# Query weights loaded by eight DMAs of 16 rows each, every eighth partition, in place of one DMA of 128 rows

## The chip, the cores and the metric

The kernel runs on one core of a Trainium2 chip. The metric is the time of one execution on the device, in microseconds (us). A core has TensorE (PE), which multiplies matrices, VectorE (DVE), ScalarE (ACT), GpSimd (POOL) and SyncE (SP); SyncE does nothing here but issue transfers. Transfers run on 16 DMA engines beside the five. The on-chip memory has 128 partitions; a tile's row lies in one partition.

## The reference: one decode step of attention, then a gated feed-forward block

There are four sequences with one new token each, 512 features, 32 heads of 128, and a cache of 8192 keys and values for each head. All tensors are bf16.

```python
h  = x + attention(layernorm(x), k_cache, v_cache, wq, wo)
h2 = h + w_down @ (sigmoid(w_gate @ n) * (w_up @ n))     # n = layernorm(h)
# attention: q = layernorm(x) @ wq; softmax(q k^T / sqrt(128)) v; @ wo
```

The caches are 256 MB each, every byte is read once, and each is used for one query alone. The query weights wq are 512 x 4096, which is 4 MB.

## The kernel before, in words

The kernel is written engine by engine, with a list of operations for each engine and semaphores between them; nothing is reordered by a scheduler. A small helper class collects the lists: `emit` (line 41) adds an instruction with its waits, and `dma` (line 74) adds a transfer, which raises its semaphore by 16 when it has landed.

**Memory.** The largest tile, KV (line 126), has three slots of 64 KB in each partition. Slot 1 first holds x, slot 2 first holds wq, and slot 0 receives the first keys. Row p of wq's part of slot 2 is four consecutive rows of the matrix wq, 32 KB in one piece (line 179): partition p holds features 4p to 4p+3.

**Start.** ACT's queue loads x (line 178), and SyncE's queue loads wq (line 179). TensorE transposes x (line 227), VectorE, TensorE and ScalarE form the layer norm (lines 201 to 222), and TensorE projects the query with 128 small matmuls (line 239), once wq has landed. Line 249 spreads the query over partitions, line 255 copies it out, and GpSimd writes it, masked, into the left operand Lq (line 266).

**The main loop.** A group g is one sequence and four heads; there are 32. A key load (line 276) and a value load (line 290) bring 8 MB each, as 128 rows of 64 KB. VectorE transposes the keys in place in eight pieces (line 321), TensorE forms the scores (line 331), VectorE and ScalarE the softmax (lines 341 to 360), and TensorE multiplies with the values of the group before (line 370). Turns three to 31 of TensorE and VectorE run as a loop in hardware.

**Order of the transfers.** All but x go through SyncE's one queue, in this order: wq, keys 0, keys 1 (waits for the transposes of x, whose slot they take), values 0 (wait for the projection, as they take the slot of wq), keys 2, and then values and keys in turns, each waiting for the slot that it takes to become free (`load_k`, line 272, and `load_v`, line 278). The weights of the output projection and of the feed-forward block follow at the end (lines 298 to 315), and the result is stored last (line 512).

**End.** Output projection (line 409), second layer norm, gate and up projections (line 489), down projection (line 505), and a last transpose by matmul (line 510).

Of the kernel before, what the change touches and what calls it, by code (L numbers as in the profile page):

```python
# [88 lines left out]
def bass_sequential_preLN__mha_block_cached__glu_gated_glu__decode_kernel(  # L89
# [13 lines left out]
    _, H, S, DH = A_k_cache.shape  # L103
    F = B_w_gate.shape[1]
    assert DH == 128 and H == 32 and D == 512 and F == 14 * 128 and B == 4 and S == 8192
    NDC = D // 128
# [3 lines left out]
    SLOT = 4 * S * DH // 128  # L110
# [5 lines left out]
    prog = _Prog()  # L116
    emit = prog.emit

    with ExitStack() as es:
        def SB(name, shape, dt, **kw):  # L120
            return es.enter_context(nc.sbuf_tensor(name, shape, dt, **kw))

        def raw(t):
            return t.tensor if hasattr(t, "tensor") else t

        KV = SB("KV", [128, 3, SLOT], BF16, align_bytes=256)
# [29 lines left out]
        KVROW = 3 * SLOT  # L156

        def kv(slot, off, inner, p0=0, np_=128):
            return bass.AP(raw(KV), p0 * KVROW + slot * SLOT + off, [[KVROW, np_], *inner])
# [10 lines left out]
        for k in keys:  # L170
# [5 lines left out]
            "h (p r) d -> (h p) (r d)", p=32)  # L176

        t_x = prog.dma("act", "x", lambda e: e.dma_start(x_bf, A_x.rearrange("b s d -> (b s) d")))
        t_wq = prog.dma("sp", "wq", lambda e: e.dma_start(
            kv(2, 0, [[1, NDC * H * DH]]), A_wq.rearrange("(p c) f -> p (c f)", p=128)))  # L180

        t_id0 = emit("pool", lambda e: e.memset(ident[:, :], 0.0))
        t_ident = emit("pool", lambda e: e.affine_select(
# [386 lines left out]
```

## Time and profile before

| | |
|---|---|
| median of three runs | 1278.9 us (1278.86 to 1279.51) |
| profiled execution, first to last instruction | 1277.6 us |
| the profile's mean transfer rate | 431 GB/s over the span |
| read from the chip's main memory | 550.77 MB |
| mean granted TensorE clock | 0.912 of full speed |
| VectorE transposing keys (L321) | 568.6 us in 256 instructions |
| TensorE matmuls of scores (L331) | 543.2 us in 2048 |
| TensorE matmuls with values (L370) | 433.2 us in 1984 |

The runs' time includes what lies around the span; of the profiled execution itself the span is what is recorded, 1.3 us under the median of the runs.

How to read the profile. It is taken from one execution by the hardware. Its slices cut the span into 40 equal parts and give each engine's busy share in tenths; the row "DMA" gives the mean busy share of the 16 DMA engines. The queue table names the queues: q1 is SyncE's, q10 is ACT's, q8 and q14 fetch instructions and tables. A packet is one contiguous row that one DMA engine moves, or the small write that reports the end of a DMA on one engine. The stretches table takes parts of the span that the reader chooses and gives for each its bounds, its length, each engine's busy time and number of instructions, the granted clock, the DMA share (1.00 is all 16 engines) and the rate in GB/s; a packet counts whole in the stretch in which it starts. Timeline rows begin with start and length in us, and end with what ended the engine's idle time. "SPq" is SyncE's queue of instructions.

### The profile page before, as it was taken

The numbers are of one execution on the slowest core, as the hardware profiler recorded it, in microseconds if no ns is written. First come the engines' busy times: TensorE is split into PE (matmuls) and PEld (weight loads), VectorE is DVE, ScalarE is ACT, GpSimd is POOL, SyncE is SP. The second block draws the span as 40 slices with busy tenths as digits, with TensorE's granted clock in tenths as the row PEclk, the third lists the DMA queues.
The fourth block names the chain that finished last, engine by engine and source line by source line (L and its number), as shares of the span: only waits on it lengthen the run. The fifth ranks groups of instructions, "written<-read, shape, count | busy, mean of one in ns | idle before, by whom it ended". The sixth has DMA issues, their size and how long they took to land. (4 is left out here: it accounts for less than half of the span.)

```text
span 1277.6 us, 11138 instructions
## 1 busy us (share of the span) xinstructions
PE 1002.2 (78%) x4553; PEld 416.0 (33%) x4553; DVE 698.6 (55%) x729; ACT 84.8 (7%) x204; POOL 20.6 (2%) x84
## 2 busy tenths in 40 slices
PE   1598777779777788777788777797777797777898
PEld 1233323333223333223333333333233333333335
DVE  0855665446655446654456654456654466554461
ACT  0000000000000000000000000000000000000010
POOL 1000000000000000000000000000000000000000
PEclk9899888899888898888998888998888998889987
DMA  9999999999999999999999999999999999999998
GB/s 423 429 424 433 427 446 429 431 435 433 439 429 437 429 443 431 435 431 437 437 429 435 433 439 431 435 431 441 433 431 435 433 437 431 437 429 441 431 427 352
DMA packets 11605, 550.95 MB, mean 431 GB/s; under 512 B 1220, under 2 KB 1480, under 8 KB 2888
## 3 DMA queue, kind: packets, MB, share of 16 engines
q1 hardware_dynamic: 11584, 550.77, 99.6%
q8 instruction: 8, 0.13, 0.0%
q14 instruction: 5, 0.04, 0.0%
q10 hardware_dynamic: 8, 0.00, 0.0%
HBM read 550.77 MB, written 0.00 MB: 431 GB/s over the span
## 5 line engine op out<-in xcount | busy, mean ns | idle before, releaser
L321 DVE STREAM_TRANSPOSE KV<-KV 128x2048 uint32<-128x2048 uint32 x256 | 568.6, 2279 | 381.6 <-DVEq L52 381.6
L331 PE MATMUL PS<-KV,Lq 128*128 128x512 bf16 x2048 | 543.2, 416 | 259.1 <-PEq L52 258.4
L370 PE MATMUL PS<-KV,PT 128*128 128x512 bf16 x1984 | 433.2, 379 | 0.0
L331 PEld LDWEIGHTS PS<-KV,Lq 128*128 128x128 bf16 x2048 | 199.5, 104 | 602.2 <-issue 443.2
L370 PEld LDWEIGHTS PS<-KV,PT 128*128 128x128 bf16 x1984 | 193.9, 98 | 234.4
L347 ACT ACTIVATE E_sb<-PS,TS 128x512 bf16<-128x512 f32 x32 | 22.0, 688 | 1124.9 <-DVE TS L346 1124.9
L341 DVE TENSOR_REDUCE TS<-PS 128x1 f32<-128x512 f32 x32 | 22.1, 692 | 70.4 <-DVEq L52 70.4
L354 ACT ACTIVATE PT<-ET 32x256 bf16<-32x256 bf16 x128 | 53.0, 414 | 30.9 <-DVE ET L350 28.5
L350 DVE STREAM_TRANSPOSE ET<-E_sb 128x512 bf16<-128x512 bf16 x32 | 22.8, 711 | 30.7 <-DVEq L52 30.7
L396 DVE STREAM_TRANSPOSE OX<-PS 128x512 f32<-128x512 f32 x32 | 21.7, 677 | 21.0 <-PE PS L384 12.3
L266 POOL TENSOR_TENSOR Lq<-q_all,mask 128x16 bf16<-128x16 bf16 x32 | 8.4, 264 | 574.9 <-DVE TS L346 563.3
L270 POOL COPY OT<-OTs 128x4 bf16<-128x4 bf16 x30 | 5.8, 194 | 623.6 <-DVE OTs L399 623.6
L384 PE MATMUL PS<-KV,PT 128*128 128x512 bf16 x64 | 14.0, 379 | 0.0
L239 PE MATMUL PS<-xnT,KV 128*128 128x4 bf16 x128 | 3.6, 166 | 9.3 <-DMA KV<-in_A_wq_dram 9.3
L342 DVE STREAM_TRANSPOSE TS<-TS 128x32 f32<-128x32 f32 x32 | 6.8, 212 | 4.7
L359 DVE STREAM_TRANSPOSE TS<-TS 128x32 f32<-128x32 f32 x32 | 6.8, 211 | 4.7
L346 DVE STREAM_TRANSPOSE TS<-TS 128x32 f32<-128x32 f32 x32 | 6.8, 211 | 4.7
L399 DVE TENSOR_SCALAR OTs<-Or,small 128x4 bf16<-128x4 f32 x30 | 6.9, 229 | 4.5 <-DVEq L52 0.6
L384 PEld LDWEIGHTS PS<-KV,PT 128*128 128x128 bf16 x64 | 6.3, 98 | 7.5
L344 DVE TENSOR_SCALAR TS<-small 128x32 f32<-128x32 f32 x32 | 5.8, 181 | 5.0 <-DVEq L52 0.6
L358 DVE COPY TS<-small 128x32 f32<-128x32 f32 x32 | 5.8, 181 | 4.7
L398 DVE TENSOR_REDUCE Or<-OX 128x4 f32<-128x16 f32 x32 | 5.7, 179 | 4.7
(68 smaller groups left out, 77.0 us busy)
## 6 DMA issues: line engine op xcount, KB each, us to landing
KV<-in_A_v_cache_dram SPq DMA_DIRECT2D x2, 4096.0 KB, 27.4
KV<-in_A_wq_dram SPq DMA_DIRECT2D x1, 4096.0 KB, 12.3
KV<-in_A_wo_dram SPq DMA_DIRECT2D x1, 3072.0 KB, 22.5
KV<-in_B_w_gate_dram SPq DMA_DIRECT2D x1, 1792.0 KB, 28.2
KV<-in_B_w_up_dram SPq DMA_DIRECT2D x1, 1792.0 KB, 23.7
KV<-in_A_wo_dram SPq DMA_DIRECT2D x1, 1024.0 KB, 24.6
KV<-in_B_w_down_dram SPq DMA_DIRECT2D x1, 1024.0 KB, 23.1
KV<-in_A_k_cache_dram SPq DMA_DIRECT2D x32, 32.5
```

The costliest lines, as they stand in the source:

```text
L266: emit("pool", lambda e: e.tensor_tensor(dst, src, msk, ALU.mult), [t_q, t_mk, t_lq0, t_a5.get(g - 1), t_oc.get(g - 3)], key="lq")
L321: emit("dve", lambda e: e.transpose(v, v), key="tp", take=take, keep=keep)
L331: ins = e.matmul(S_b[0], Lq[:, hp, 15 - s:15 - s + 128], rhs, start=(s == 0 and hp == 0), stop=(s == NS - 1 and hp == 3))
L341: dv(lambda e: e.tensor_reduce(TS[:, 0, 0:1], S_b[0], AX.X, ALU.max), [t_ts0] if g == 0 else [], [("sc", 1)])
L342: dv(lambda e: e.transpose(TS[:, 1, :], TS[:, 0, :]))
L347: emit("act", lambda e: e.activation(E_sb[:, :], S_b[0], ACT.Exp, bias=TS[:, 3, 0:1], scale=SCALE, accum_out=TS[:, 4, 0:1]), [t_a5[g]], ke ...
L350: t_et[g] = dv(lambda e: e.transpose(ET[:, :], E_sb[:, :]), take=[("ex", 1)], key="dve")
L354: emit("act", lambda e, dst=dst, src=src: e.activation(dst, src, ACT.Copy), [t_et[g], t_pt0], key="pt")
L370: ins = e.matmul(O_b, PT[:, u3, off:off + 128], rhs, start=(j == 0 and rl == 0), stop=(j == 3 and rl == NS - 1))
L384: ins = e.matmul(V_b, PT[:, u3, off:off + 128], rhs, start=(j == 0 and rl == 0), stop=(j == 3 and rl == NS - 1))
L396: emit("dve", lambda e: e.transpose(OX[:, :, :].rearrange("p (r i) x -> p r i x", r=4), src), w, key="dv", take=take, keep=keep)
L399: t_ox[g] = emit("dve", lambda e: e.tensor_scalar(dst, Or[:, :], small[:, 2 + g % 3:3 + g % 3], None, op0=ALU.mult), take=[("dv", 1)], kee ...
```

## The change

The load of wq is written as eight loads. Load r (0 to 7) takes partitions r, 8+r, 16+r, ... 120+r of slot 2, one row of 32 KB for each, and the same rows of the matrix. All eight go through SyncE's queue one behind the other, ahead of the first key load, and raise the same semaphore by 16 each; the projection waits for the last value, 128 in place of 16. Every row of wq ends in the partition in which it was before. No other instruction is changed, and the order of the instructions on all engines stays.

```diff
-        t_wq = prog.dma("sp", "wq", lambda e: e.dma_start(
-            kv(2, 0, [[1, NDC * H * DH]]), A_wq.rearrange("(p c) f -> p (c f)", p=128)))
+        for r in range(8):
+            t_wq = prog.dma("sp", "wq", lambda e, r=r: e.dma_start(
+                bass.AP(raw(KV), r * KVROW + 2 * SLOT, [[8 * KVROW, 16], [1, NDC * H * DH]]),
+                A_wq.rearrange("(p r c) f -> r p (c f)", p=16, r=8)[r]))
```

## The prediction

> **What bounds the kernel now.** I read the page's slices and queue table first, because one transfer is changed; then the list of DMA issues, SyncE's timeline, and last the stretches table, cut to the length of one "round": the time in which each of the 16 DMA engines moves one row.
>
> ```profile
> DMA  9999999999999999999999999999999999999998
> DMA packets 11605, 550.95 MB, mean 431 GB/s; under 512 B 1220, under 2 KB 1480, under 8 KB 2888
> q1 hardware_dynamic: 11584, 550.77, 99.6%
> q10 hardware_dynamic: 8, 0.00, 0.0%
> PE 1002.2 (78%) x4553; PEld 416.0 (33%) x4553; DVE 698.6 (55%) x729; ACT 84.8 (7%) x204; POOL 20.6 (2%) x84
> ```
>
> The DMA engines are full in every slice (9 means 90% or more), and SyncE's queue q1 alone takes 99.6% of their time, while TensorE is busy for 78% and VectorE for 55%. So the transfers set the time. Before I believe that a delay in them reaches the end, I want to see that they never pause.
>
> ```profile
> core 0: us, PE busy (x) PEld busy (x) DVE busy (x) ACT busy (x) POOL busy (x), PEclk, DMA share, GB/s
> 0.00:1.70 1.70, 0.00 (x0) 0.00 (x0) 0.17 (x1) 0.37 (x1) 0.85 (x7) 1.00 0.00 1
> 1.70:3.50 1.80, 0.55 (x6) 0.46 (x6) 0.57 (x4) 0.91 (x1) 1.44 (x8) 1.00 1.05 292
> 3.50:4.70 1.20, 0.34 (x2) 0.24 (x2) 0.58 (x4) 0.21 (x2) 1.20 (x1) 1.00 1.01 437
> 4.70:5.91 1.21, 0.00 (x0) 0.00 (x0) 0.35 (x2) 1.21 (x1) 1.21 (x1) 1.00 1.00 433
> ...
> 10.75:11.96 1.21, 0.00 (x0) 0.00 (x0) 0.00 (x0) 0.00 (x0) 0.00 (x0) 1.00 1.00 433
> 11.96:14.38 2.42, 1.26 (x47) 1.26 (x48) 0.00 (x0) 0.00 (x0) 0.00 (x0) 1.00 1.00 433
> 14.38:16.80 2.42, 2.32 (x87) 2.23 (x84) 0.06 (x1) 0.00 (x0) 0.00 (x0) 1.00 1.00 433
> ...
> 20.00:1240.00 1220.00, 963.54 (x3997) 390.05 (x3998) 691.92 (x698) 78.24 (x193) 14.01 (x61) 0.91 1.00 434
> 1240.00:1270.00 30.00, 29.25 (x271) 17.30 (x269) 3.73 (x15) 3.57 (x8) 1.30 (x6) 0.91 0.99 418
> 1270.00:1277.60 7.60, 4.65 (x142) 4.29 (x139) 0.67 (x3) 0.22 (x1) 0.00 (x0) 0.50 0.40 155
> ```
>
> The last two columns matter. A packet is counted where it starts, and every packet of wq is a row of 32 KB (4 MB over 128 rows). Nothing is moved until 1.7 us. The first round starts there and takes about 1.8 us, and from 3.5 us on there are seven rounds of 1.21 us: 16 rows of 32,768 B in 1.21 us are 433 GB/s, 27.1 GB/s for each engine. The cache rows of 64 KB that follow take 2.42 us a round, at the same 433. That the rate doesn't depend on the size of the row, and is still 434 over 1220 us with a share of 1.00, tells me two things: it is the fixed width of some path and not a latency, and there is no pause anywhere in which a delay could be absorbed.
>
> ```profile
> 0.74 0.40 SPq L179 DMA_DIRECT2D KV<-in_A_wq_dram  x1
> 1.19 1.71 SPq L276 DMA_DIRECT2D KV<-in_A_k_cache_dram  x2
> 16.73 0.33 SPq L290 DMA_DIRECT2D KV<-in_A_v_cache_dram  x1
> 2.25 0.29 PE L227 MATMUL PS<-ident,KV 4*128 4x4 bf16 x4 [2.25 <-POOL mask L192]
> KV<-in_A_wq_dram SPq DMA_DIRECT2D x1, 4096.0 KB, 12.3
> KV<-in_A_k_cache_dram SPq DMA_DIRECT2D x32, 32.5
> KV<-in_A_v_cache_dram SPq DMA_DIRECT2D x31, 34.4
> out_dram<-KV SPq DMA_DIRECT2D x1, 4.0 KB, 1.4
> ```
>
> These are SyncE's issues (start, length), TensorE's transposes of x, and the times from issue to landing. A cache load of 8.39 MB moves in 19.3 us at 434 GB/s, but takes 32.5 or 34.4 us to land: it always stands behind another one. So a microsecond added to the wq transfer moves every later transfer by a microsecond, the end too.
>
> **The change part by part.** One instruction of 128 rows goes; eight of 16 rows come. The bytes, the partition of every row, the place in the queue and the semaphore stay; TensorE waits for 128 on it in place of 16. Load r brings partitions r, 8+r, ... 120+r.
>
> *Issue.* A load costs SyncE 0.33 to 0.40 us (the first and third row of the last fence), so eight end by 0.74 + 8 x 0.40 = 3.9 us, 2.8 us later than now, and the first cache load is issued there. The transfer of wq covers this: its own rows last until 12 us, so the queue runs dry only if issuing took three times as long. Load r is issued by 0.74 + 0.40 r and begins no earlier than round r, at 1.7 + 1.2 r. The second cache load also waits for TensorE's transposes of x, done by 2.6 us, so it follows at once. Cost: nothing.
>
> *Completions.* Rows in the code give 10,384 packets on q1, and 75 DMAs with 16 completions each give 1,200: together the 11,584 of the table. The output store is one of the 75 and has 16 rows, so a DMA of 16 rows already uses 16 engines; x, with 4 rows on ACT's queue, has 8 packets, four rows and four completions. So each new load puts one row on each engine. There are 7 x 16 more completions. What one costs shows where two loads meet:
>
> ```profile
> 31.38:33.79 2.41, 0.00 (x0) 0.00 (x0) 0.05 (x1) 0.00 (x0) 0.00 (x0) 1.00 1.01 435
> ```
>
> This is the round in which the second cache load begins behind the completions of the first, and it runs at 435. Seven such seams cost nothing that I can see.
>
> *The rounds themselves.* Today the hardware chooses which 16 rows move together, and they run at 433. After the change each round is dictated: 16 partitions, eight apart. If the path of fixed width is at the sender (each engine's own 27.1 GB/s), nothing changes. If it is at the receiver, with several partitions behind one entrance, the set of rows decides: 16 rows on 16 entrances take 1.21 us; 16 rows on eight entrances, two at each, have to bring 64 KB through each one, and that is what a cache round does in 2.42 us. The trace of before has no bulk transfer of fewer than 128 partitions, so the price is bounded by these two rows: nothing below (a round can't beat 1.21 us, since both sizes run at the same full rate), and 2.42 - 1.21 = 1.21 us a round above, 8 x 1.21 = 9.7 us in all. The ends are far apart. I take the upper one, because the uniform 433 at two sizes is what a fixed entrance gives, and because eight is the one spacing that makes all 16 numbers agree in their lowest three bits, the most regular pattern that address bits can be made to collide on.
>
> [...]
>
> *What is late next.* The projection, now released at 13.1 us, is released near 22.8 us.
>
> ```profile
> 13.12 3.58 PE L239 MATMUL PS<-xnT,KV 128*128 128x4 bf16 x128 [9.28 <-DMA KV<-in_A_wq_dram]
> 17.83 0.26 POOL L266 TENSOR_TENSOR Lq<-q_all,mask 128x16 bf16<-128x16 bf16 x1 [11.55 <-DVE q_all L255]
> 33.74 17.67 DVE L321 STREAM_TRANSPOSE KV<-KV 128x2048 uint32<-128x2048 uint32 x8 [15.99 <-DVEq L52]
> ```
>
> The query is ready at 18.1 us, 15.6 us ahead of the first cache load's landing at 33.7; both move together, so this slack stays. Value load 0, issued at 16.7 behind the projection, moves to 26.4; two cache loads (38.6 us) stand ahead of it in the queue, so it isn't missed.
>
> *Sum.* Own span 1277.6 + 9.7 = 1287.3 us. The three timed runs have a median of 1278.9, 1.3 us over the span; with that, **1288.6 us**.
>
> **The rivals.**
>
> *A, not slower: the width is at the sender, or the rounds are already such.* Then all eight rounds stay at 1.21 us and the time is 1278.9. For it: the 27.1 GB/s could as well be each engine's own, and no row here separates the two. Against it: only the regular spacing, and that the hardware's present choice is clean. It decides if the load lands near 12.3 us after its issue. A gain is bounded by the start: rows could flow at most 1.0 us sooner (1.7 less 0.74) and the first round could shrink by 0.6 us, 1.6 us in all, 1277.3 at best, still within 0.2%.
>
> *B, half: pairs drift apart.* If the first four loads use one half of the entrances and the last four the other half, and the engine that comes first at an entrance keeps it, the pair overlaps: one waits four rounds, and eight follow. That is 12 rounds for 8, 4 x 1.21 = 4.8 us, 1283.7. [...] Against it: two equal streams of packets that arrive together should be served in turns.
>
> *C, slower in another way: each load pays its own start and end.* The nearest row is the store of 4 KB, 1.4 us from issue to landing. Paid in line by the seven added loads that is 9.8 us, 1288.7: the same time, from another cause; the gaps between loads would then be empty, where in my forecast the engines stay busy. Against it stands the seam at 31.4 us. [...]
>
> *D, the change doesn't spread:* a load of 16 rows on fewer engines. With eight engines used in every load the price would be that of the forecast; with one, 4.19 MB at 27.1 GB/s would take 155 us and end near 1424. The packet count above speaks against both.
>
> **How the numbers follow.** Chances: forecast 0.62 (1288.6; its own range 1287 to 1290), A 0.19 without a gain and 0.02 with one beyond the bound, B and anything between 0.11 (1281.5 to 1287), C 0.04, D 0.02. Each case that costs is over 0.2% (2.6 us, about what a measurement of this kernel can tell from no change): slower 0.79, same 0.19, faster 0.02. Leaving A out would leave out over 2 in 10, so the range reaches down to it: 1278.5 to 1290.5.
>
> **What would show it.** Right: wq's rounds at 2.42 us and 217 GB/s with the DMA share still 1.00; last landing near 22.8 us in place of 13.1; the first transpose of keys near 43.4 us; q1 with 11,696 packets; from there on every stretch at 434 and the same gaps as now, 9.7 us later. Wrong at the price: rounds at 1.21 us (A), or a mixture (B). Wrong at the cause: rounds at 1.21 us with an empty DMA share between them (C). Wrong at the consequence: the landing 9.7 us late, but the end not, which needs a pause in the DMA share after 20 us that I don't see now.

## The result, and the profile after

| | before | after |
|---|---|---|
| median of the runs | 1278.92 us (5 runs) | 1289.22 us (5 runs, 1289.06 to 1289.35) |
| span of the profiled execution | 1277.6 us | 1287.4 us |
| ratio after to before | | 1.0079, 95% interval 1.0068 to 1.0090 |

The change makes the kernel 10.3 us slower. The forecast was 1288.6 us. In two of the kernels below (the two halves of the memory, and the reading side) one run of four took some 8 us longer than the other three, which widens their intervals; all times are medians.

The queue table and the first slices of the profile after, to be read against those of before: the bytes are the same, q1 has 112 packets more, which are 7 loads x 16 completions, and the DMA engines are again busy in every slice. But the first slice moves only 267 GB/s, where it moved 423. The rates of before:

```profile
GB/s 423 429 424 433 427 446 429 431 435 433 439 429 437 429 443 431 435 431 437 437 429 435 433 439 431 435 431 441 433 431 435 433 437 431 437 429 441 431 427 352
```

And the lines of after:

```profile
DMA  9999999999999999999999999999999999999998
GB/s 267 448 422 430 444 424 434 444 424 436 442 426 436 442 426 436 442 426 436 440 428 436 440 428 436 440 428 436 440 428 436 440 428 436 440 426 436 440 418 360
q1 hardware_dynamic: 11696, 550.77, 99.7%
```

The stretches of the first 22 us, cut to the new rounds (last two columns: DMA share and GB/s):

```profile
4.00:6.55 2.55, 0.00 (x0) 0.00 (x0) 0.75 (x5) 1.49 (x2) 2.27 (x2) 1.00 1.01 206
...
11.65:14.05 2.40, 0.00 (x0) 0.00 (x0) 0.00 (x0) 0.00 (x0) 0.00 (x0) 1.00 1.00 218
...
19.15:21.70 2.55, 0.00 (x0) 0.00 (x0) 0.00 (x0) 0.00 (x0) 0.00 (x0) 1.00 1.01 206
30.00:1250.00 1220.00, 963.14 (x3997) 390.10 (x3998) 691.81 (x698) 78.17 (x193) 13.91 (x61) 0.92 1.00 434
```

This is the pattern to learn: the DMA engines are fully busy, and yet they move 206 GB/s. A round of 16 rows takes 2.55 us in place of 1.21. Nothing is idle, so no wait and no issue explains it; the packets themselves are slow: in the traces, each row of the second to the eighth round takes 2.39 to 2.56 us, where it took 1.21 to 1.22. As soon as the cache loads run, the rate is 434 GB/s again.

The timeline of the issues and of the steps behind wq:

```profile
0.74 5.04 SPq L180 DMA_DIRECT2D KV<-in_A_wq_dram  x8
5.82 1.05 SPq L278 DMA_DIRECT2D KV<-in_A_k_cache_dram  x2
23.60 3.57 PE L241 MATMUL PS<-xnT,KV 128*128 128x4 bf16 x128 [19.85 <-DMA KV<-in_A_wq_dram]
44.36 17.66 DVE L323 STREAM_TRANSPOSE KV<-KV 128x2048 uint32<-128x2048 uint32 x8 [16.14 <-DVEq L52]
```

(Lines after the load are numbered two higher than before.) The projection starts 10.5 us later than at 13.12 us, the first transposes of keys 10.6 us later than at 33.74 us, and the span ends 9.8 us later.

### The profile page after: what moved, and what is told of

It reads as the page before. It is cut to its first block, busy times and chain, and to the rows that moved or that the text cites. A ratio compares the mean times of both kernels' runs of the same rounds, so it can differ in the third digit from the quotient of the medians.

```text
span 1287.4 us, 11145 instructions
## 1 busy us (share of the span) xinstructions
PE 1001.6 (78%) x4553; PEld 415.9 (32%) x4553; DVE 698.4 (54%) x729; ACT 84.7 (7%) x204; POOL 20.5 (2%) x84
## 3 DMA queue, kind: packets, MB, share of 16 engines
q1 hardware_dynamic: 11696, 550.77, 99.7%
## 5 line engine op out<-in xcount | busy, mean ns | idle before, releaser
L241 PEld LDWEIGHTS PS<-xnT,KV 128*128 128x128 bf16 x128 | 3.5, 104 | 19.9 <-DMA KV<-in_A_wq_dram 19.9
```

Source lines behind the costliest of these rows:

```text
L241: ins = e.matmul(XB[:, B * h:B * (h + 1)], kv(2, c * H * DH + h * DH, [[1, DH]]), cols(xnT, c), start=(c == 0 and h == 0), stop=(c == NDC ...
```

## The experiments

**The theories.** E (entrances) supposes that the rows of a round share paths of fixed width into the on-chip memory, that each path, an "entrance", serves a group of partitions, and that "every eighth partition" uses only half of the paths. Its rivals: N (each load has a price of its own), S (one row for each engine and load is what is slow), Q (the reading side: which rows of the matrix are read together), and later F (an engine is slow when it writes to partitions other than its usual ones, those of a 128-row load). How many entrances there are, which partitions share one, and which engine writes to which partition, no trace or run here shows: where the expectations count entrances, the count is my assumption, and what the runs give is the time of each set of partitions. Each kernel below is the kernel before with another load of wq (the last four have extra loads ahead of it); times are medians beside the kernel before on the same chip.

### Many loads, all partitions

```diff
+        for r in range(8):   # w = an eighth of a row, 4 KB
+            dma_start(kv(2, r * w, [[1, w]]), wq_rows[:, r * w:(r + 1) * w])
```

> Eight loads again, but each has all 128 partitions and an eighth of the columns (4 KB a row). Theory E (entrances: groups of partitions share a path of fixed width, and the 16 rows of a round crowd on half of the paths): each round is again the hardware's own choice of rows, so about 433 GB/s, wq's landing near 13.1 to 13.6 us, time 1278.9 to 1279.6. Theory N (number of loads: each of eight loads pays about 1.3 us of its own): landing near 23 us and time near 1289. Theory S (one row for each engine and load is what is slow): like E here.

Measured: 1279.23 us against 1278.96 (ratio 1.0003, interval 0.9993 to 1.0013), projection from 13.01 us. Eight loads in a row cost nothing that can be told from no change. Theory N falls.

### Sixteen neighbouring partitions in each load

```diff
+        for r in range(8):   # partitions 16r to 16r+15, one row each
+            dma_start(KV[16r : 16r+16], wq_rows[16r : 16r+16])
```

> Eight loads of 16 rows, but partitions 16r to 16r+15 in place of every eighth. Theory E, if neighbouring partitions share an entrance: the 16 rows have only four entrances, a round takes four times 1.21 us, 4.8 to 5.1 us, wq's landing near 43 us, time 1308 to 1310. [...] Theories N and S: as with every eighth partition, 1289. Theory Q (the reading side: which rows of the matrix are read together): no figure, but no reason for exactly twice the price of every eighth partition.

Measured: 1304.68 us against 1278.96 (1.0201, interval 1.0184 to 1.0218), projection from 39.18 us. One stretch of this kernel, as long as one round; the next six run at 116 GB/s as well:

```profile
4.50:9.02 4.52, 0.00 (x0) 0.00 (x0) 0.35 (x2) 1.39 (x2) 1.78 (x2) 1.00 1.00 116
```

The number of loads, rows and bytes is that of the change, and the price is 2.5 times as high. That decides against S, by which the two had to be equal. The round is 4.52 us and not the 4.8 to 5.1 of theory E, and the time 3.3 us under its range. The four entrances of that forecast were assumed; the runs show a round 3.7 times as long as the 1.21 us of before, and why not four times stays open.

### Two halves of the memory

```diff
+        for p0 in (0, 64):
+            dma_start(KV[p0 : p0+64], wq_rows[p0 : p0+64])
```

> Two loads of 64 rows, partitions 0 to 63 and 64 to 127: four rows for each engine and load. Theory E, if the halves of the memory have separate entrances: half of them are used at a time, rounds of 2.4 to 2.55 us, landing near 23 us, time 1288.6 to 1289.5. Theory N: one load more costs 1.3 us, time near 1280. Theory S: four rows for each engine in a load, so at most a quarter of the price, time 1279 to 1281.5.

Measured: 1289.90 us against 1278.96 (1.0105, interval 1.0072 to 1.0137), projection from 24.21 us. One of its stretches, as long as one round:

```profile
4.10:6.65 2.55, 0.00 (x0) 0.00 (x0) 0.78 (x6) 1.49 (x2) 2.19 (x2) 1.00 1.01 206
```

Two loads with four rows for each engine cost what the change's eight loads cost. The split into small loads isn't what is slow; half of the partitions at a time is enough. This is theory E's figure again (0.4 us over its range), and S's is missed by 8 us.

### Every seventh partition

```diff
+        for r in range(7):   # partitions r, r+7, ... r+105
+            dma_start(KV[r : r+106 : 7], wq_rows[r : r+106 : 7])
+        dma_start(KV[112:128], wq_rows[112:128])
```

> Seven loads of 16 rows, every seventh partition (0 to 111), and one of the last 16. As many loads, rows and bytes as with every eighth. [...] Theories N and S: as with every eighth partition, 1289, all packets near 2.5 us.

Measured: 1288.41 us against 1278.96 (1.0075, interval 1.0058 to 1.0091). That is 0.6 us under N and S; E gives no time here, as that would need to know which partitions share an entrance. Three stretches:

```profile
5.90:8.10 2.20, 0.00 (x0) 0.00 (x0) 0.00 (x0) 0.00 (x0) 0.37 (x2) 1.00 1.01 238
10.10:11.60 1.50, 0.00 (x0) 0.00 (x0) 0.00 (x0) 0.00 (x0) 0.00 (x0) 1.00 1.10 350
15.90:19.20 3.30, 0.00 (x0) 0.00 (x0) 0.00 (x0) 0.00 (x0) 0.00 (x0) 1.00 1.13 159
```

The first seven loads run at 238 to 350 GB/s, faster than the change's 206, and the last load, on 16 neighbours, is slowest, at 159. Against N and S stands that not all packets are near 2.5 us: in the single packets of the trace, all 16 rows of the second and of the third round took 2.0 to 2.3 us. But none of them kept the 1.21 us of before either. So either all these rows share entrances, or rows that share nothing are held up as well, or something else slows rows on unusual partitions, such as F. This open question is what the last four runs are for.

### Four sets of every fourth partition, four of every second

```diff
+        for q in range(4):   # partitions 32+q, 36+q, ... 92+q
+            dma_start(KV[32+q : 93+q : 4], wq_rows[32+q : 93+q : 4])
+        for p0 in (0, 1, 96, 97):   # every second partition of 0-31 and of 96-127
+            dma_start(KV[p0 : p0+31 : 2], wq_rows[p0 : p0+31 : 2])
```

> Eight loads of 16 rows, one row for each engine and load, as in the change; only the sets differ. Loads 0 to 3 take every fourth partition of 32 to 95, loads 4 to 7 every second one of 0 to 31 and of 96 to 127. [...] Theory S (one row for each engine and load is what is slow): all eight rounds 2.5 us, time 1289.

Measured: 1285.89 us against 1278.97 (1.0052, interval 1.0035 to 1.0069). Its stretches show the two kinds of sets in one kernel:

```profile
4.00:7.00 3.00, 0.00 (x0) 0.00 (x0) 0.87 (x6) 1.49 (x2) 2.27 (x2) 1.00 1.07 371
7.00:8.50 1.50, 0.00 (x0) 0.00 (x0) 0.00 (x0) 0.00 (x0) 0.00 (x0) 1.00 1.28 415
8.50:11.00 2.50, 0.00 (x0) 0.00 (x0) 0.00 (x0) 0.00 (x0) 0.00 (x0) 1.00 1.19 249
11.00:13.50 2.50, 0.00 (x0) 0.00 (x0) 0.00 (x0) 0.00 (x0) 0.00 (x0) 1.00 0.95 210
```

One row for each engine and load runs at 371 to 415 GB/s where the 16 rows lie on every fourth partition of 32 to 95, and falls to 210 when the sets change to every second one of 0 to 31 and 96 to 127. Against S (1289 us) this is 3 us.

### Eight rows in each load

```diff
+        for h in range(4):
+            for q in range(4):   # partitions 32h+q, 32h+q+4, ... 32h+q+28
+                dma_start(KV[32h+q : 32h+q+29 : 4], wq_rows[32h+q : 32h+q+29 : 4])
```

> Sixteen loads of eight rows, every fourth partition of one quarter; eight engines at most, 16 rounds each. Theory E: eight rows on eight entrances, 1.21 us a round in the first eight (partitions 0 to 63), then 2.4 us, because by then the other eight engines bring keys to the entrances of 64 to 127; wq's landing near 32 us, time 1296 to 1299. Theory S: 2.5 us in all 16 rounds, landing near 43 us, time near 1310. If the load is spread over 16 engines after all, neither.

Measured: 1298.10 us against 1278.97 (1.0152, interval 1.0135 to 1.0169), projection from 32.36 us. Three stretches:

```profile
3.50:10.00 6.50, 0.35 (x2) 0.25 (x2) 0.93 (x6) 1.49 (x2) 2.77 (x2) 1.00 0.48 202
10.00:12.90 2.90, 0.00 (x0) 0.00 (x0) 0.00 (x0) 0.00 (x0) 0.00 (x0) 1.00 0.55 237
16.00:30.00 14.00, 0.00 (x0) 0.00 (x0) 0.00 (x0) 0.00 (x0) 0.00 (x0) 1.00 0.98 213
```

A DMA share of 0.48 with 202 GB/s is half of the engines at nearly full speed, 26 GB/s each. From 16 us on a share of 0.98 brings 213 GB/s: now the other engines move keys, by theory E to the same entrances, and all 16 together are as fast as the eight were alone. The single packets of the trace agree: most rows of wq take 1.21 us in the first eight rounds and 2.4 to 2.6 us from 16 us on, and the key rows beside them 4.9 to 5.0 us between 18 and 28 us, where a key row alone takes 2.42. One number doesn't tell these two states apart (both are near 210 GB/s); the share beside it does.

### The reading side changed alone

```diff
-                A_wq.rearrange("(p r c) f -> r p (c f)", p=16, r=8)[r]))
+                A_wq.rearrange("(p c) f -> p (c f)", p=128)[16 * r:16 * r + 16]))
```

> As the change on the writing side (every eighth partition), but load r reads the 16 neighbouring rows 16r to 16r+15 of the matrix in place of every eighth; so the rows of wq land in other partitions than those that the projection expects, and the output is another. Theory E: nothing changes against the change, rounds of 2.4 to 2.55 us, time 1289 to 1289.6. Theory Q (which rows of the matrix are read together sets the price): rounds of 1.21 us and 1279, or at least a price clearly off 10 us.

Measured: 1289.00 us against 1278.97 (1.0099, interval 1.0064 to 1.0134), with a span of 1287.3 us; the change has 1287.4. What is read together doesn't matter here. Q falls.

### Thirty-two rows in each load

```diff
+        for r in range(4):   # partitions r, r+4, ... r+124
+            dma_start(KV[r : r+125 : 4], wq_rows[r : r+125 : 4])
```

> Four loads of 32 rows, every fourth partition, two rows for each engine. [...] Theory E: if each engine gets two consecutive rows (8e+r, 8e+4+r) or rows 16 apart, each round has eight entrances, 2.4 to 2.55 us, time 1289; if each engine gets the two rows of one entrance, 1.21 us, time 1279 to 1280. Theory S: two rows for each engine, so half the price at most, time near 1284.

Measured: 1279.34 us against 1278.97 (1.0003, interval 0.9993 to 1.0012). Its stretches are those of the kernel before, as this one shows:

```profile
5.10:6.31 1.21, 0.00 (x0) 0.00 (x0) 0.00 (x0) 0.81 (x1) 1.17 (x2) 1.00 1.01 433
```

S, near 1284, falls. Of the divisions that the expectation names, two consecutive rows for an engine would make rounds of every eighth partition, and rows 16 apart rounds within one half of the memory; both took 2.55 us where they were measured, so both are out. How the load is divided instead no trace shows. Four loads of every fourth partition are free; eight of every eighth cost 10 us.

### Extra loads, to price one set of partitions by itself

In these four the load of wq is that of before. Ahead of it stand five extra loads of 16 rows into parts of KV that are overwritten later; `p0` and `step` choose the partitions.

```diff
+        for slot, half in ((0, 0), (0, 1), (1, 0), (1, 1), (2, 1)):   # p0, step as below
+            t_ext = dma_start(KV[p0 : p0+15*step+1 : step, slot, half],
+                              wq_rows[p0 : p0+15*step+1 : step])
...
-            w = [] if g == 0 else [t_xT] if g == 1 ...   # what key load g waits for
+            w = [t_ext] if g == 0 else [t_xT] if g == 1 ...
```

With p0 = 32 and step 4 (every fourth partition of 32 to 92):

> The kernel before, with five extra loads of 16 rows (32 KB a row) ahead of its 128-row load of wq; the first key load waits for them. All five take every fourth partition of 32 to 92. Theory E: 16 entrances, rounds of 1.21 us, 6.1 us for the five and up to 0.4 us for the later start, time 1285 to 1285.5. [...]

With p0 = 11 and step 7 (every seventh partition of 11 to 116):

> [...] Theory E: rounds of 1.21 us, as with every fourth partition of 32 to 92, time 1285 to 1285.5. Theory F: rounds of 2.4 us or more, time 1291 to 1292.

With p0 = 28 and step 4 (every fourth partition of 28 to 88):

> [...] Theory E with independent engines: 14 engines at 1.21 us a row, two at 2.55 us, and as every later load ends with its slowest engine, time 1291 to 1292.5. Theory E with coupling (an engine that waits at a shared entrance holds up others): rows of the 14 near 1.5 us, a slowest engine that is less late, time 1286.5 to 1290.

With p0 = 4 and step 8 (every eighth partition of 4 to 124):

> [...] Theory E: rounds of 2.55 us, 12.8 us for the five and up to 0.4 us for the start, time 1291.5 to 1292.3.

| partitions | time | ratio to before (1279.00), interval | first 7.3 us of transfers |
|---|---|---|---|
| every 4th from 32 | 1286.24 us | 1.0055 (1.0038 to 1.0072) | 350 GB/s |
| every 7th from 11 | 1286.20 us | 1.0056 (1.0039 to 1.0072) | 355 GB/s |
| every 4th from 28 | 1291.99 us | 1.0101 (1.0084 to 1.0118) | 319 GB/s |
| every 8th from 4 | 1291.64 us | 1.0098 (1.0082 to 1.0115) | 216 GB/s |

The stretch from 1.7 to 9 us, in the order of the table, one kernel in each fence; for the last two also the issue of the key loads, which waits for the landing of the extra loads:

```profile
1.70:9.00 7.30, 0.89 (x6) 0.71 (x6) 1.50 (x10) 2.40 (x3) 4.23 (x9) 1.00 0.98 350
```

```profile
1.70:9.00 7.30, 0.88 (x6) 0.70 (x6) 1.50 (x10) 2.39 (x3) 4.22 (x9) 1.00 0.99 355
```

```profile
1.70:9.00 7.30, 0.88 (x6) 0.70 (x6) 1.50 (x10) 2.40 (x3) 4.22 (x9) 1.00 0.98 319
18.27 0.81 SPq L281 DMA_DIRECT2D KV<-in_A_k_cache_dram  x2
```

```profile
1.70:9.00 7.30, 0.88 (x6) 0.70 (x6) 1.50 (x10) 2.40 (x3) 4.23 (x9) 1.00 1.03 216
16.15 0.81 SPq L281 DMA_DIRECT2D KV<-in_A_k_cache_dram  x2
```

The first two are equal, 0.04 us apart, where F had the second 5 us and more above E's time for the first. So F falls, as far as engines write to their usual partitions in the first and to others in the second; that was my assumption, and no trace shows it. The fourth gives the change's price again: 12.6 us for five loads, 2.5 us each, where the free sets cost 7.2 us, less than 1.5 us each. The third is the surprise of practical use. The set moved down by four partitions, from 32 to 92 to 28 to 88, makes the kernel pay as much as for every eighth partition, though the rate in the stretch is hardly lower (319 GB/s after 350). I read it so: a few engines are late, and each later load ends with its slowest engine. The key loads' issue bears this out: the extra loads have landed at 10.82 and 11.52 us in the two free kernels, at 16.15 us with every eighth partition, and last, at 18.27 us, with every fourth from 28. The single packets of that trace show how: between 3.9 and 9 us the slow rows take 2.5 to 2.7 us, and then 2.8 to 4.1 us, three at a time. The 14 engines and two of that forecast rest on an assumed count; the packets of its second round show 13 rows and three. Which partitions these rows belong to isn't shown. Rows of wq's own 128-row load are among the slow ones (below), so this price includes the load that follows. The cost is that of the slowest rows, not of the average.

The free sets were 0.7 us above their expectation (1285.5). What adds this to loads of 16 rows stays open.

## Why the prediction was right

*What bounds the kernel.* Right. Where all engines are late alike, the delay of the projection reaches the end: 10.5 us late for 10.3 us of time in the change, 26.1 for 25.7 with 16 neighbours, 19.2 for 19.1 with eight rows, 11.1 for 10.9 with two halves. With the extra loads on every fourth partition from 28 it is 14.6 for 13.0: there only three engines are late (in the trace, rows of wq move three at a time after 21.1 us), and the rest is lost to the spread named under the sum or to the queue of the others; no run tells which.

*Issue and completions cost nothing.* Right in the sum: eight loads over all partitions cost 0.3 us, which can't be told from no change. The eight issues took 5.04 us and not 8 x 0.40 = 3.2; the first key load was issued at 5.82 us, still almost 16 us before its first rows could move.

*The price of a round.* The choice of the upper end was right, and its size a little too low: 2.55 us a round, not 2.42. A round brings 16 x 32,768 B in 2.55 us, 206 GB/s, 5% less than half of the 433 of before. Seven rounds cost 9.2 us more than before (17.70 us in place of 8.46), where 8.5 were forecast; the first round and the landing of the last rows make it 10.5.

*What is late next.* Right: projection, keys and values moved together; the first transposes were 10.6 us late where 9.7 were forecast.

*The sum.* 9.7 us forecast, 9.8 in the span; in the medians 10.3, as 1.8 us lie around the span where 1.3 were taken over from before. Part of the agreement is luck, as 10.6 us of delay at the first transposes became 9.8 at the end. From the first transposes to the end the kernels of this study take between 1242.9 and 1244.4 us, the kernel before 1243.9 and the change 1243.0, with no relation to the price of wq that I can see; what spreads them stays open.

*The rivals.* A was wrong, B too: all 16 rows of a round stay equally slow, round after round at 206 GB/s (2.51 to 2.56 us a row), with one round, the fifth, at 218 (2.39 to 2.41 us); why that one is faster no run shows. C had nearly the right time with the wrong cause; the DMA share of 1.00 between the loads speaks against it at once, and the kernel with eight loads over all partitions decides. D is excluded by q1's 11,696 packets.

*The choice.* Of my two reasons for the upper end, the uniform 433 decides nothing, as engines of fixed width (A) give it too. The other, three equal low bits, isn't the rule: every eighth partition from 4 costs 2.5 us a load, as in the change, but sets of every fourth partition are free from 32 on and dear from 28 on. As far as these two reasons go, the right choice was luck. Which partitions share an entrance stays open: the runs give the price of the sets that were tried, and E, with no map of its own, orders them only after the fact.

*Where theory E falls short.* It gives no time for every seventh partition, and the free sets cost 0.7 us more than it had. The single packets also show rows that are slowed only a little beside others that are slowed much. With partitions 28 to 88, between 11.5 and 15.5 us, 13 engines write rows of wq's 128-row load, and every one of these rows takes 1.50 us where the kernel before took 1.21, beside three rows of 4.0 to 4.1 us. In the second round of the same kernel, though, 13 rows took 1.21 to 1.23 us beside three of 2.6 to 2.7. When rows are held up, and by what, stays open.

## What to carry to other kernels

Before a load is cut by partitions, write down which partitions move together in one round of 16 rows, and measure that set. Here every eighth partition cost 10.3 us, two halves 10.9 and 16 neighbours 25.7, and three slow rows in a round were enough for 13.0; cutting the load by columns, or into sets of every fourth partition over all 128, cost nothing that could be measured. A DMA share of 1.00 says that engines are occupied, not that they are fast (206 GB/s and 434 both stood beside it); the rate has to be read too. In a kernel whose transfers never pause, a few microseconds at the start are paid at the end: 10.5 us here became 10.3.

## What was unexpected of the hardware

- Five small loads of every fourth partition from 28 cost as much (13.0 us) as five of every eighth from 4 (12.6 us), with a 128-row load behind them, where every fourth from 32 cost 7.2 us.
- SyncE's issue of eight loads in line took 5.04 us with 16 rows eight partitions apart, 3.62 us with 16 neighbouring rows and 3.82 us with 128 rows cut by columns; the one load of 128 rows took 0.40 us. Fewer rows aren't issued faster, and what sets the time stays open.
- Sixteen rows eight partitions apart moved at 206 GB/s, 5% less than half of the 433 of a round before.
